# A gated dilated convolution on one core: one VectorE instruction put ahead of another, some products and half an output piece moved forward, and four stores in place of two

## The chip, the cores and the metric

The kernel runs on one core of one Trainium2 chip. The metric is device microseconds (us) of one execution; the time given for a kernel is the median of its runs.

## The reference

`x` has 2 batches of 16000 rows of 256 channels, in bf16. Three taps with a dilation of two rows make 512 channels from them; the first half goes through a tanh and the second through a sigmoid, the two are multiplied, and a 256 by 256 matrix makes the output.

```python
B, T, D, K = (2, 16000, 256, 3)
xp = pad(x, 4 rows ahead)
h = xp[t+4] @ w[0] + xp[t+2] @ w[1] + xp[t] @ w[2]
z = tanh(h[..., :256]) * sigmoid(h[..., 256:])
out = z @ w_o
```

## The kernel before, in words

**Tiles.** Rows are handled in groups. One group and two remainders (`extra`, `end`) of plain form compute the three taps directly (`direct`, L292). The other 15 groups are wide: 256 positions of 8 rows each, whose sums and differences (`q`, `qp`, `qm`, `qd`, made by VectorE and GpSimd at L213 to L231) let 14 products of 512 columns do the work of 24. Every group has four blocks, one for each 128 of the 512 channels, in the order tanh, sigmoid, tanh, sigmoid.

**A block.** A wide block B owns one `y` tile in PSUM (two banks, from a ring of three) and goes through these steps. `first` (L254, two products) fills bank 0 and ScalarE keeps it as `st` (`keep_first`, L276). `second` (L260, two products) adds to bank 0, and ScalarE keeps it as half of `sv` (`keep_second`, L280); GpSimd makes the other half of `sv` (`other`, L283). `third` (L263, two products) adds to bank 0, and VectorE makes bank 1 from bank 0 and `st` (`split_bank`, L286, called the split below). `late(B, 0)` (L268, four products) adds to both banks. VectorE subtracts `y` from `sv` (`rest`, L290). `late(B, 1)` (L271, four products) adds the last terms to both banks. ScalarE applies the function to `sv` (L332) and to `y` (L334). After two blocks VectorE multiplies tanh by sigmoid (the gate, L339).

**Output pieces.** A group's `z` gives pieces of 256 output rows each: `out_mm` (L364) does four products of 256 columns into one bank of the two-buffer ring `ps_o`, ScalarE evicts it to half of an `osb` tile (L401), and when both halves are there SyncE stores 256 KB (L374 or L381).

**Order of the work.** The whole order is written out by hand; each engine runs its instructions in program order, and the waits between engines follow from the tiles. The loop at L529 has one slot for each wide block, k = 4 to 63; slot 4 is called the first slot, slot 5 the second, slot 7 the fourth. In slot k TensorE does `late(V, 0)` of the block before (V), `second` of the slot's block (B), in the first six slots some products of the remainders (`extra_block`, L459, into `e_ps` tiles of the ring `ps_o`, two blocks of four still to come in slots 6 and 7; `plain_ends`, L467, in slots 8 and 9), then the output pieces that are due (`project`, L523: none up to slot 6, one in slots 7 to 9, two after), `first` of the next block (N), `third` of B, the other half of `first`, and `late(V, 1)`. Slot 5 (`early_second`) begins with `second` and holds both parts of `first` together.

VectorE's order within a slot: what `small` and `big` list for it (sums, differences, gates), `rest(V)`, in slot 7 alone one more sum from the list `mid` (L573; the sum `qm` of the next group, `wide_m`, L222), then the split of B; in slot 7 the gate of `extra` follows (L591). `other(B, last)` and the quarter differences (L234) on GpSimd wait for VectorE's latest listed instruction.

**The end.** Behind the loop (L613 on) come `late` of the last block, `project(2)`, and then four pieces of the group before, in two pairs (`left`): the first pair goes to a `y` tile and is evicted by VectorE, the second goes to `ps_o` and is evicted by ScalarE; each pair is stored in one transfer of 256 KB. Between and behind them stand the last gates (L620) and the last group's eight pieces, each stored singly (128 KB, L649), from both SyncE's and ScalarE's queue.

Of the kernel before, what the change touches and what calls it, by code (L numbers as in the profile page):

```python
# [13 lines left out]
def kernel(  # L14
# [37 lines left out]
    TAPS = (2, 0, 1)  # L52
# [16 lines left out]
    end = dict(wide=False, b=B - 1, r0=T // 4 - RE, R=RE, g="z")  # L69
    for g, G in enumerate(groups):  # L70
        G["g"] = g
    wides = [G for G in groups if G["wide"]]
    XW = RW + RH * max(len(G["parts"]) for G in wides)

# [13 lines left out]
    def new_y():  # L88
        return ps_y.tile([P, 2, BANK], f32, name="y")
# [8 lines left out]

    def load_plain(G):
        b, r0, R = G["b"], G["r0"], G["R"]  # L100
        xt = G["x"] = xt_pool.tile([P, 4, CT, RH + R], bf16, name=f"xt{G['g']}")
        if r0 == 0:
            nc.gpsimd.memset(xt[:, :, :, RH - 1:RH], 0.0)
            return
        nc.sync.dma_start_transpose(
            out=xt[:].rearrange("p j ct r -> p (j ct) r"),
            in_=x[b, 4 * (r0 - RH):4 * (r0 + R), :].rearrange("(r j) c -> r (j c)", j=4),
        )
# [142 lines left out]
    def first(B, ct):  # L251
        if ct == 0:
            B.y = new_y()
        nc.tensor.matmul(  # L254
            B.y[:, 0, :], lhsT=W["wmh"][:, ct, B.osl], rhs=B.G["qp"][:, :, ct, :],
            start=ct == 0, stop=ct == CT - 1, skip_group_check=True,
        )
# [4 lines left out]
    def third(B):  # L262
        mm(B, W["wm"], B.G["qm"][:, 1], 0)  # L263

    def late(B, n):
        G = B.G
        if n == 0:
            mm(B, W["wt"], G["q"][:, 1, 0], 0)  # L268
            mm(B, W["wu"], G["q"][:, 1, 1], 1)
        else:  # L270
            mm(B, W["wd2"], G["qd"][:, 0], 0)  # L271
            mm(B, W["wd0"], G["qd"][:, 1], 1)
# [12 lines left out]
    def split_bank(B):  # L285
        nc.vector.scalar_tensor_tensor(  # L286
            out=B.y[:, 1, :], in0=B.st[:], scalar=-0.5, in1=B.y[:, 0, :], op0=ALU.mult, op1=ALU.add)
# [67 lines left out]
            return G["z"][:, dt, WIDE_PLACE[jp], lo:lo + P]  # L355
        return G["z"][:, dt, 2 * jp + q, rb0:rb0 + P]

    def out_mm(G, rb0, jp, o_ps=None):
        if o_ps is None:
            o_ps = ps_o.tile([P, 2, D], f32, name="o_ps", tag="o_ps")  # L360
        G["o", rb0, jp] = o_ps
        for q in range(2):
            for dt in range(NT):
                nc.tensor.matmul(  # L364
                    o_ps[q] if isinstance(o_ps, list) else o_ps[:, q, :], lhsT=z_columns(G, rb0, jp, q, dt), rhs=wo_sb[:, dt, :],
                    start=(dt == 0), stop=(dt == NT - 1),
                )

    def store(G, rb0, js, osb, queue=None):

        queue = queue or nc.sync
        if not G["wide"]:
            t0 = 4 * G["r0"] + 4 * rb0
            queue.dma_start(out=out[G["b"], t0:t0 + 4 * P, :].rearrange("(p j) d -> p j d", j=4)[:, js, :], in_=osb[:])  # L374
            return
        row = 0
        for b, t0, rows in G["parts"]:
            lo, hi = max(rb0, row), min(rb0 + P, row + rows)
            if lo < hi:
                t = t0 + 8 * (lo - row)  # L380
                queue.dma_start(  # L381
                    out=out[b, t:t + 8 * (hi - lo), :].rearrange("(p j) d -> p j d", j=8)[:, js, :],
                    in_=osb[lo - rb0:hi - rb0],
                )
            row += rows

    def out_evict(G, rb0, jp, on_dve):
        o_ps = G["o", rb0, jp]
        copy = nc.vector.tensor_copy if on_dve else nc.scalar.copy
        if jp is None:  # L390
            te = 4 * G["r0"]
            osb = consts.tile([P, 2, D], bf16, name="osb_end")
            copy(out=osb[:], in_=o_ps)
            rows = out[G["b"], te:te + 4 * RE, :].rearrange("(r q h) d -> h r q d", q=2, h=2)
            for h in range(2):
                nc.sync.dma_start(out=rows[h], in_=osb[h * RE:(h + 1) * RE])
            return
        h = jp % 2
        if h == 0:
            G["osb"] = osb_pool.tile([P, 4, D], bf16, name="osb")  # L400
        copy(out=G["osb"][:, 2 * h:2 * h + 2, :], in_=o_ps)  # L401
        if h == 1:
            store(G, rb0, slice(2 * jp - 2, 2 * jp + 2), G["osb"])


    blocks = [Block(G, oi) for G in groups for oi in range(4)]
    extras = [Block(extra, oi) for oi in range(4)]
    ends = [Block(end, oi) for oi in range(4)]
    ND = 4
# [47 lines left out]
    last = wide_m(G0, 1)  # L457

    def extra_block(i, taps):  # L459
        E = extras[i]  # L460
        if TAPS[0] in taps:
            E.y = ps_o.tile([P, BANK], f32, name="e_ps", tag="o_ps")
        direct(E, taps, E.y[:])
        if TAPS[-1] in taps:
            activate(E, E.y[:])
# [17 lines left out]
    ready, todo, made = [], [], []  # L483
    small, big, mid = {}, {}, {}

    def do(steps, k):
        ins = None
        for step in steps.pop(k, []):
            ins = step() or ins
        return ins  # L490
# [32 lines left out]
    def project(n):  # L523
        for piece in todo[:n]:
            out_mm(*piece)
            made.append(piece)
        del todo[:n]

    for k in range(ND, NB):  # L529
        B, V = blocks[k], (blocks[k - 1] if k > ND else None)  # L530

        E = {
            ND: [(0, TAPS[2:]), (1, TAPS[:1])], ND + 1: [(1, TAPS[2:])], ND + 2: [(2, TAPS)],
            ND + 3: [(3, TAPS)],
        }.get(k, [])
        early_second = k == ND + 1
        if early_second:
            second(B)
            keep_second(B)
            extra_block(1, TAPS[1:2])  # L540
        if V:
            late(V, 0)
        if k >= ND + 2:
            Y = blocks[k - 2]
            activate(Y, "y")
            note_gates(Y, k)
        last = do(small, k) or last

        if k == ND + 6:
            todo.append(ready.pop())  # L550
        big_late = k == ND + 1

        def big_and_quarter(last):
            last = do(big, k) or last
            if B.oi == 0 and k > ND:
                quarter(B.G, 3, last)
            elif B.oi and not big_late and B.G["n"] + 1 < len(wides):
                for i in range(0 if k == ND + 2 else B.oi - 1, B.oi):
                    quarter(wides[B.G["n"] + 1], i, last)
            return last  # L560

        if not big_late:
            last = big_and_quarter(last)
        if not early_second:
            second(B)
            keep_second(B)
        if k == ND:
            for i in range(2, ND):
                activate(blocks[i], bank(blocks[i], i))
        other(B, last)  # L570
        if V:
            rest(V)
        last = do(mid, k) or last  # L573
        for e in E:
            extra_block(*e)
        if k in (ND + 4, ND + 5):
            plain_ends(*((ACT.Sigmoid, 1) if k == ND + 5 else (ACT.Tanh, 0)))

        project(0 if k < ND + 3 else 1 if k < ND + 6 else 2)
        evict()  # L580
        N = blocks[k + 1] if ND < k < NB - 1 else None

        split_first = k >= ND + 2
        if N:
            first(N, 0)
            if not split_first:
                first(N, 1)
        third(B)
        split_bank(B)
        if k == ND + 3:  # L590
            last = gates_of(extra, slice(0, 2))  # L591
        if big_late:
            last = big_and_quarter(last)
        if V:
            activate(V, "sv")
        if N:
            if split_first:
                first(N, 1)
            keep_first(N)
        if V:  # L600
            late(V, 1)
        todo += ready
        ready.clear()
        if B.oi == 0:
            if loaded_wide < len(wides):
                load_wide(loaded_wide)
                loaded_wide += 1
            if k == ND:
                load_end()
# [2 lines left out]

    Y, V = blocks[NB - 2:]  # L613
    G = V.G
    late(V, 0)
    activate(Y, "y")
    big.pop(NB)
# [5 lines left out]
    gate_phases(0, slice(0, 2), nc.gpsimd)  # L623
    rest(V)
    gate_phases(0, slice(2, 4))
    project(2)
    evict()


# [5 lines left out]
    left = [todo[i:i + 2] for i in range(0, len(todo), 2)]  # L635
# [17 lines left out]

    activate(V, "sv")
    two_pieces(left[0], "y")
    out_evict(*left[0][0], True)
    late(V, 1)
    gate_phases(1, slice(2, 4))
    activate(V, "y")
    out_evict(*left[0][1], True)  # L660
    two_pieces(left[1], "o")
    last_mm(0, (1, 2), "y")
    gate_phases(1, slice(0, 2))
    out_evict(*left[1][0], False)
    out_evict(*left[1][1], False)
    last_mm(P, (1, 2), "y")
    last_evict(0, (1, 2), (nc.sync, nc.sync))
    last_mm(0, (0, 3), "o")
# [35 lines left out]
```

## Time and profile before

| | |
|---|---|
| median of 3 runs | 263.51 us (263.49 to 263.56) |
| the profiled execution | 263.43 us |
| its span, first to last instruction | 261.6 us |
| mean granted TensorE clock | 0.996 |
| TensorE matmul busy | 256.0 us (98%) |
| ScalarE busy | 245.9 us (94%) |
| VectorE busy | 226.7 us (87%) |
| GpSimd busy | 112.8 us (43%) |

Times in rows are counted from the start of the span. PE is TensorE's matmul, PEld its weight load, DVE is VectorE, ACT is ScalarE, POOL is GpSimd, SP is SyncE. A row of the timeline has the start, the length, the engine, the line, the operation, the tile written and the tiles read, and `xN` where N instructions are merged. Matmuls are pipelined: the length of a row runs to the end of its last matmul, while the next one starts earlier, so the distance between the starts is what TensorE needs. On the other engines too a row can begin a few hundredths before the end of the one ahead of it.

### The profile page before, as it was taken

How to read it: one execution, taken by the hardware profiler on the slowest of the kernel's cores; microseconds unless marked ns; L12 is line 12 of the kernel's file. 1: busy time of each engine (PE TensorE's matmuls, PEld its weight loads, DVE VectorE, ACT ScalarE, POOL GpSimd, SP SyncE). 2: the span in 40 equal slices, each digit the busy share in tenths (PEclk: the TensorE clock that was granted, in tenths of full speed). 3: DMA queues.
4: the chain of work that ended last, by engine and by line, in shares of the span. 5: the costliest groups of instructions: out<-in, count | busy, mean ns of one | idle time of the engine just before them, and what ended most of it. 6: DMA issues, size and time to landing. Idle time of an engine off the chain costs nothing.

```text
span 261.6 us, 4231 instructions
## 1 busy us (share of the span) xinstructions
PE 256.0 (98%) x1464; PEld 144.2 (55%) x1464; DVE 226.7 (87%) x264; ACT 245.9 (94%) x378; POOL 112.8 (43%) x129
## 2 busy tenths in 40 slices
PE   8999999999999999999999999999999999999993
PEld 6644555555555555555555555555555555555562
DVE  2989969989889989999988988988988988986673
ACT  4668789999999999999999999999999999999993
POOL 1033434454453454355455355355345345444240
PEclk9999999999999999999999999999999999999998
DMA  7979073292834719256392934729274491221226
GB/s 209 201 177 192 0 180 94 83 209 83 175 119 123 209 52 212 111 117 174 96 175 105 199 120 103 203 79 215 81 169 124 101 231 43 80 83 40 82 80 241
DMA packets 79109, 35.10 MB, mean 134 GB/s; under 512 B 69232, under 2 KB 71536, under 8 KB 79088
## 3 DMA queue, kind: packets, MB, share of 16 engines
q1 hardware_dynamic: 77984, 33.92, 52.8%
q10 hardware_dynamic: 1104, 0.92, 1.1%
q8 instruction: 11, 0.18, 0.3%
q14 instruction: 10, 0.08, 0.1%
HBM read 1.18 MB, written 16.38 MB: 67 GB/s over the span
## 4 chain that ended last, share of the span: by engine, by line
PE 93%; DVE 3%; issue 1%; DMA 1%; ACT 0%; DVEq 0%; ACTq 0%
PE y L246 58%; PE o_ps L364 19%; PE y L254 9%; PE y L310 2%; PE y L140 1%; PE e_ps L310 1%; PE f_ps L310 1%; DVE sv L290 1%; DVE y L286 1%; DMA out_dram<-osb 1%; DVE qm L222 1%; PE wt_ps L171 0%; ACT osb L401 0%; PE y L364 0%; DVE osb L648 0%
## 5 line engine op out<-in xcount | busy, mean ns | idle before, releaser
L283 POOL TENSOR_TENSOR sv<-sv,st 128x512 f32<-128x512 f32 x60 | 76.4, 1274 | 23.9 <-ACT sv L280 22.2
L231 POOL TENSOR_TENSOR qd<-xq 128x256 bf16<-128x256 bf16 (+2 forms) x60 | 34.9, 585 | 114.2 <-DVE zw L339 55.4
L290 DVE TENSOR_TENSOR sv<-sv,y 128x1024 f32<-128x1024 f32 x60 | 72.7, 1212 | 3.8 <-PE y L246 3.7
L246 PE MATMUL y<-qd,wd_sb 128*128 128x512 bf16 x240 | 61.6, 379 | 0.1
L401 ACT CAST osb<-o_ps 128x512 bf16<-128x512 f32 x114 | 61.1, 591 | 0.2 <-PE o_ps L364 0.2
L286 DVE SCALAR_TENSOR_TENSOR y<-st,y 128x512 f32<-128x512 f32 x60 | 41.8, 696 | 21.9 <-PE y L246 19.6
L364 PE MATMUL o_ps<-wo_sb,zw 128*128 128x256 bf16 x450 | 58.4, 273 | 0.0
L364 PEld LDWEIGHTS <-zw 128*128 128x128 bf16 x480 | 47.0, 98 | 17.1
L254 PE MATMUL y<-qp,wmh_sb 128*128 128x512 bf16 x120 | 44.8, 379 | 0.0
L246 PEld LDWEIGHTS <-wd_sb 128*128 128x128 bf16 x240 | 23.5, 98 | 28.5 <-issue 0.6
L280 ACT ACTIVATE sv<-y 128x512 f32<-128x512 f32 x60 | 35.9, 598 | 1.4 <-PE y L246 1.1
L213 DVE TENSOR_TENSOR q<-xq 128x2048 bf16<-128x2048 bf16 (+2 forms) x32 | 36.8, 1155 | 0.0
L276 ACT ACTIVATE st<-y 128x512 f32<-128x512 f32 x60 | 36.3, 607 | 0.2 <-PE y L254 0.2
L246 PE MATMUL y<-q,wt_sb 128*128 128x512 bf16 x120 | 35.7, 379 | 0.2 <-DVE y L286 0.2
L246 PE MATMUL y<-qm,wph_sb 128*128 128x512 bf16 x120 | 35.7, 379 | 0.0
L246 PE MATMUL y<-qm,wm_sb 128*128 128x512 bf16 x120 | 35.7, 379 | 0.0
L246 PE MATMUL y<-q,wu_sb 128*128 128x512 bf16 x120 | 35.7, 379 | 0.0
L339 DVE TENSOR_TENSOR zw<-thw,sgw 128x2048 bf16<-128x2048 bf16 x28 | 34.1, 1217 | 0.0
L332 ACT ACTIVATE thw<-sv 128x1024 bf16<-128x1024 f32 x30 | 32.4, 1078 | 0.4 <-DVE sv L290 0.4
L332 ACT ACTIVATE sgw<-sv 128x1024 bf16<-128x1024 f32 x30 | 32.4, 1078 | 0.0
L334 ACT ACTIVATE sgw<-y 128x1024 bf16<-128x1024 f32 x30 | 31.3, 1043 | 0.1
L334 ACT ACTIVATE thw<-y 128x1024 bf16<-128x1024 f32 x30 | 31.3, 1044 | 0.0
(68 smaller groups left out, 178.8 us busy)
## 6 DMA issues: line engine op xcount, KB each, us to landing
out_dram<-osb SPq DMA_DIRECT2D x56, 256.0 KB, 2.1
out_dram<-osb SPq DMA_DIRECT2D x6, 128.0 KB, 2.2
w_sb<-in_w_dram ACTq DMA_DIRECT2D x2, 256.0 KB, 4.4
out_dram<-osb SPq DMA_DIRECT2D x2, 160.0 KB, 2.0
osb<-in_x_dram SPq DMA_DIRECT2D x1, 256.0 KB, 3.2
w_sb<-in_w_dram SPq DMA_DIRECT2D x1, 256.0 KB, 4.3
xq<-in_x_dram SPq DMA_TRANSPOSE x16, 7.2
out_dram<-osb ACTq DMA_DIRECT2D x2, 128.0 KB, 2.2
```

Of the source, the lines that this page charges most:

```text
L213: ins = nc.vector.tensor_tensor(out=sums(G, "q")[:, h, :, :, :, sl].rearrange("p h q ct r -> p h (q ct) r"), in0=s, in1=a, op=ALU.subtract ...
L246: nc.tensor.matmul(B.y[:, bank, :], lhsT=wmat[:, ct, B.osl], rhs=mv[:, :, ct, :], start=False, stop=ct == CT - 1, skip_group_check=True,)
L254: nc.tensor.matmul(B.y[:, 0, :], lhsT=W["wmh"][:, ct, B.osl], rhs=B.G["qp"][:, :, ct, :], start=ct == 0, stop=ct == CT - 1, skip_group_che ...
L276: nc.scalar.mul(B.st[:], B.y[:, 0, :], 4.0)
L280: nc.scalar.mul(B.sv[:, 0], B.y[:, 0, :], 2.0)
L283: after(nc.gpsimd.tensor_tensor(out=B.sv[:, 1], in0=B.sv[:, 0], in1=B.st[:], op=ALU.subtract), behind)
L286: nc.vector.scalar_tensor_tensor(out=B.y[:, 1, :], in0=B.st[:], scalar=-0.5, in1=B.y[:, 0, :], op0=ALU.mult, op1=ALU.add)
L290: nc.vector.tensor_tensor(out=B.sv[:], in0=B.sv[:], in1=B.y[:], op=ALU.subtract)
L332: nc.scalar.activation(out=dst[:, 2:4, :], in_=B.sv[:], func=func, scale=0.25)
L334: nc.scalar.activation(out=dst[:, 0:2, :], in_=B.y[:], func=func, scale=0.25)
L364: nc.tensor.matmul(o_ps[q] if isinstance(o_ps, list) else o_ps[:, q, :], lhsT=z_columns(G, rb0, jp, q, dt), rhs=wo_sb[:, dt, :], start=(dt ...
L401: copy(out=G["osb"][:, 2 * h:2 * h + 2, :], in_=o_ps)
```

## The change

There are four edits. (1) In slot 7 `do(mid, k)`, which is the sum `wide_m`, stands behind `split_bank(B)` instead of ahead of the remainder's products. (2) In slot 5 one half of `first` of block 6 (one product) stands ahead of `late(V, 0)`; the other half stays where it was. Of the remainder's block 2 the two products of the first tap stand at the end of slot 5, behind `third`, and of block 3 the two products of the first tap stand in slot 6; slots 6 and 7 do what is left of these blocks. (3) Behind the loop, half of the first output piece (two products of 256 columns) stands ahead of the last block's `late(V, 0)`, and its other half behind it. (4) The four pieces in `left` are stored singly as soon as each is evicted, 128 KB each.

```diff
-    def out_mm(G, rb0, jp, o_ps=None):
+    def out_mm(G, rb0, jp, o_ps=None, qs=(0, 1)):
...
-        for q in range(2):
+        for q in qs:
...
-    def out_evict(G, rb0, jp, on_dve):
+    def out_evict(G, rb0, jp, on_dve, single=False):
...
-        if h == 1:
+        if single:
+            store(G, rb0, slice(2 * jp, 2 * jp + 2), G["osb"][:, 2 * h:2 * h + 2])
+        elif h == 1:
             store(G, rb0, slice(2 * jp - 2, 2 * jp + 2), G["osb"])
...
-            ND: [(0, TAPS[2:]), (1, TAPS[:1])], ND + 1: [(1, TAPS[2:])], ND + 2: [(2, TAPS)],
-            ND + 3: [(3, TAPS)],
+            ND: [(0, TAPS[2:]), (1, TAPS[:1])], ND + 1: [(1, TAPS[2:])], ND + 2: [(2, TAPS[1:]), (3, TAPS[:1])],
+            ND + 3: [(3, TAPS[1:])],
...
             extra_block(1, TAPS[1:2])
+            first(blocks[k + 1], 0)
...
-        last = do(mid, k) or last
         for e in E:
             extra_block(*e)
...
         if N:
-            first(N, 0)
+            if not early_second:
+                first(N, 0)
             if not split_first:
                 first(N, 1)
         third(B)
+        if early_second:
+            extra_block(2, TAPS[:1])
         split_bank(B)
+        last = do(mid, k) or last
...
+    half = todo[0]
+    out_mm(*half, None, (0,))
     late(V, 0)
...
-    project(2)
+    out_mm(*half, half[0]["o", half[1], half[2]], (1,))
+    made.append(todo.pop(0))
+    project(1)
     evict()
...
-    out_evict(*left[0][0], True)
+    out_evict(*left[0][0], True, True)
...
-    out_evict(*left[0][1], True)
+    out_evict(*left[0][1], True, True)
...
-    out_evict(*left[1][0], False)
-    out_evict(*left[1][1], False)
+    out_evict(*left[1][0], False, True)
+    out_evict(*left[1][1], False, True)
```

## The prediction

> **What bounds the kernel now.** I read the page first: the busy shares and the chain of work that ended last.
>
> ```profile
> PE 256.0 (98%) x1464; PEld 144.2 (55%) x1464; DVE 226.7 (87%) x264; ACT 245.9 (94%) x378; POOL 112.8 (43%) x129
> ...
> PE 93%; DVE 3%; issue 1%; DMA 1%; ACT 0%; DVEq 0%; ACTq 0%
> ```
>
> TensorE carries 93% of the chain, so only time in which TensorE doesn't start a matmul can be won, unless matmuls go, and none do here. Next I asked for windows, to see whether the steady slots have such time: ten of them, 100.00 to 138.95.
>
> ```profile
> 100.00:138.95 38.95, 38.95 (x223) 21.52 (x221) 35.84 (x44) 38.95 (x61) 19.17 (x25) 1.00 0.68 152
> ```
>
> They have none: 38.95 of 38.95 us. A steady slot is 14 products of 512 columns and 8 of 256, which are worth 18 of 512, so ten slots are 180 such products and one takes 38.95 / 180 = 0.2164 us. I call that a unit; a product of 256 columns counts half. With it each stretch of TensorE's timeline can be checked: where two starts lie further apart than the units between them, TensorE waited. From the first slot on there are four such places of over 0.1 us, two in the second slot, one behind the fourth, one behind the loop. The end after the last matmul is stores.
>
> **The second slot.** TensorE's timeline there, then VectorE's, then one row of ScalarE's.
>
> ```profile
> 15.61 0.59 PE L246 MATMUL y<-qm,wm_sb 128*128 128x512 bf16 x2
> 16.04 0.59 PE L246 MATMUL y<-qm,wph_sb 128*128 128x512 bf16 x2
> 16.48 0.59 PE L310 MATMUL e_ps<-xte,w_sb 128*128 128x512 bf16 x2
> 17.06 0.59 PE L246 MATMUL y<-q,wt_sb 128*128 128x512 bf16 x2
> ...
> 18.79 0.59 PE L246 MATMUL y<-qm,wm_sb 128*128 128x512 bf16 x2
> 19.47 1.02 PE L246 MATMUL y<-qd,wd_sb 128*128 128x512 bf16 x4
> ```
> ```profile
> 16.31 0.69 DVE L286 SCALAR_TENSOR_TENSOR y<-st,y 128x512 f32<-128x512 f32 x1 [0.81 <-PE y L246]
> ...
> 18.19 1.22 DVE L290 TENSOR_TENSOR sv<-sv,y 128x1024 f32<-128x1024 f32 x1
> ```
> ```profile
> 15.90 0.60 ACT L336 ACTIVATE sg<-y 128x512 bf16<-128x512 f32 x1
> ```
>
> The remainder's two products (16.48) are done with at 16.48 + 2 units = 16.91; the late products start at 17.06, just behind the split (16.31 + 0.69 = 17.00). That is a wait of 0.15. `third` (18.79) ends its units at 19.22; the last late products start at 19.47, just behind `rest` (18.19 + 1.22 = 19.41), because they write the `y` that it reads. That is a wait of 0.25.
>
> The change puts one product of `first` into the first gap: the late products start at 16.91 + 0.22 = 17.13, past the split. The bank it fills is free, since the activation that read that buffer ended at 15.90 + 0.60 = 16.50; this cover is 0.41. These four units end at 18.00. Before, `rest` followed their end (17.06 + 4 units = 17.93) by 0.26, so now it starts at 18.26 and ends at 19.48, and the last late products may start 0.06 behind that, at 19.54. TensorE has until then two units of remainder 1, one of `first`, two of `third`, and the two moved products of remainder 2: 18.00 + 7 units = 19.51. So 0.03 of wait is left, the next slot starts four units later at 20.40 instead of 20.33, and two units (0.43) of its work are done. Sum: 0.43 - 0.07 = 0.36 won. The moved products issue no transfer and pass no queue. Their bank was last read by the activation of remainder 0, whose products end in the first slot. An unseen wait there is bounded by zero below and by the whole 0.36 above; I take zero, as the rows give every one of its inputs as ready.
>
> **The fourth slot.** TensorE, VectorE, GpSimd, and the same sum of VectorE's where GpSimd was idle.
>
> ```profile
> 27.91 0.59 PE L246 MATMUL y<-qm,wm_sb 128*128 128x512 bf16 x2
> 28.35 0.38 PE L254 MATMUL y<-qp,wmh_sb 128*128 128x512 bf16 x1
> 28.56 1.03 PE L246 MATMUL y<-qd,wd_sb 128*128 128x512 bf16 x4
> 29.76 0.59 PE L246 MATMUL y<-q,wt_sb 128*128 128x512 bf16 x2 [0.17 <-DVE y L286]
> ```
> ```profile
> 26.56 1.20 DVE L290 TENSOR_TENSOR sv<-sv,y 128x1024 f32<-128x1024 f32 x1
> 27.69 1.42 DVE L222 TENSOR_TENSOR qm<-q 128x1024 bf16<-128x1024 bf16 x1
> 29.03 0.68 DVE L286 SCALAR_TENSOR_TENSOR y<-st,y 128x512 f32<-128x512 f32 x1
> ...
> 31.36 1.21 DVE L290 TENSOR_TENSOR sv<-sv,y 128x1024 f32<-128x1024 f32 x1
> ```
> ```profile
> 27.29 1.27 POOL L283 TENSOR_TENSOR sv<-sv,st 128x512 f32<-128x512 f32 x1
> 31.52 0.61 POOL L231 TENSOR_TENSOR qd<-xq 128x256 bf16<-128x256 bf16 x1 [2.96 <-DVE zw L339]
> ```
> ```profile
> 14.21 0.69 DVE L222 TENSOR_TENSOR qm<-q 128x1024 bf16<-128x1024 bf16 x1
> ```
>
> The four late products (28.56) are done with at 29.43, and the next start at 29.76, behind the split, which ended at 29.71: a wait of 0.33. The split stood behind the sum (27.69, 1.42 long) though its input, `third`, was done with at 28.35. After the change the third slot starts at 20.40 and has 20 units (the moved remainder work cancels), so slot four starts at 24.73. Up to the end of `third` it has 15 units now: 27.98. In the first slot the split (16.31) followed the end of `third` (15.61 + 2 units = 16.04) by 0.27, so here it runs from 28.25 to 28.93. The slot's 20 units end at 29.06, where the next late products start without a wait; the cover is 0.07. Before it was 29.76: **0.70 won** in all, 0.15 + 0.25 + 0.33 less 0.03.
>
> What is queued behind the waiting split on VectorE: the sum, then two gates (29.71 to 31.36 before, 1.65 in all), then `rest`, for which the fifth slot's last late products wait. The sum takes 28.85 to 29.54 if it is as long as at 14.21, as GpSimd's subtraction, which follows slot four's `second`, ends 0.07 later than before, at 28.63. The gates end at 31.2, `rest` at 32.4. Ahead of those products TensorE has four late ones, two of `second`, six units of the other remainder, two of a piece and four of `first` and `third`: 29.06 + 18 units = 32.96, which is 0.56 behind `rest`; less the 0.06 that a start takes, the cover is 0.50. The sum's reader, `third` of the fifth slot, comes over two us after it. GpSimd's next instruction waits for the second gate (31.52), so it can't stand in the way between.
>
> The sum's length has two ends, 0.69 and 1.42. The 1.42 lay beside GpSimd's subtraction (27.29 to 28.56), the 0.69 beside nothing of GpSimd's; the moved sum starts behind the subtraction, so I take 0.69. With 1.42, `rest` would end at 33.13, the products would start at 33.19, 0.23 late, and the total (below) would be 263.0 instead of 262.76.
>
> The Trainium skill's page "SBUF — State Buffer", section "Who interferes with whom", says that a VectorE instruction with two SBUF inputs and a GpSimd instruction that reads SBUF exclude each other, the later one waiting for the other's end. The sum's end at 29.11, 0.55 behind GpSimd's, agrees. By that rule the sum gets its 0.69 at the new place, and the total stays.
>
> **Steady slots.** TensorE comes out of the fifth slot 0.70 ahead and needs ScalarE to follow, which was busy 38.95 of 38.95 too.
>
> ```profile
> 101.77 0.61 ACT L276 ACTIVATE st<-y 128x512 f32<-128x512 f32 x1
> ...
> 102.58 0.59 PE L246 MATMUL y<-qm,wph_sb 128*128 128x512 bf16 x2
> ```
>
> The `second` products must wait until ScalarE has read bank 0: it is done at 102.38, they start at 102.58: 0.20 of slack. In the moved slots I followed ScalarE's rows in the same way: the remainder's activations come two units earlier with their products, and its order is the same, so it keeps its distance to TensorE. I take no cost; rival (e) has the other end.
>
> **The end.** TensorE, VectorE, ScalarE, TensorE again, SyncE's issues, and the rate of the transfers (slices of 0.25 us from 252 on).
>
> ```profile
> 248.46 1.02 PE L246 MATMUL y<-qd,wd_sb 128*128 128x512 bf16 x4
> 249.48 0.59 PE L246 MATMUL y<-q,wt_sb 128*128 128x512 bf16 x2
> ```
> ```profile
> 248.73 0.70 DVE L286 SCALAR_TENSOR_TENSOR y<-st,y 128x512 f32<-128x512 f32 x1 [0.55 <-PE y L246]
> 250.60 1.22 DVE L290 TENSOR_TENSOR sv<-sv,y 128x1024 f32<-128x1024 f32 x1 [1.17 <-PE y L246]
> ```
> ```profile
> 251.94 1.07 ACT L332 ACTIVATE sgw<-sv 128x1024 bf16<-128x1024 f32 x1
> ```
> ```profile
> 253.82 1.91 PE L364 MATMUL y<-wo_sb,zw 128*128 128x256 bf16 x16
> ```
> ```profile
> 256.38 0.82 SPq L649 DMA_DIRECT2D out_dram<-osb  x2
> 258.29 0.39 SPq L649 DMA_DIRECT2D out_dram<-osb  x1
> ```
> ```profile
> GB/s 0 0 0 131 385 369 164 0 0 0 0 0 66 385 393 205 344 377 373 332 176 311 217 328 344 328 340 328 361 340 340 332 74 0 0 0 0 0 0 0
> ```
>
> TensorE is free at 248.46 + 4 units = 249.33 and waits 0.15 for the split (249.43). Half a piece is one unit: the late products start at 249.55 instead of 249.48, 0.07 late, with 0.22 done. But the last group's pieces (253.82) need the chain split, late products, `rest`, activation (done at 253.01), gate. It hangs on the late products and runs 0.07 later; the pieces, which TensorE could start 0.15 earlier, start at about 253.88. So the half piece wins nothing for those. It helps what stands between: the last four late products came 12 units behind 249.48, at 252.08, and now come as `rest` ends, at 250.67 + 1.22 + 0.06 = 251.95, so the last activation of `y`, and the ScalarE evictions behind it, start about 0.1 earlier.
>
> The single stores: SyncE issues two more, 0.39 each, ahead of the one at 256.38; nothing was moved from 253.75 to 255.00, so its queue has room there, and I cost them at nothing. The rate falls to 176 GB/s at 257.0, so the queue of transfers was nearly empty when the last seven of 128 KB came; from 257.5 to 260 they run at about 340 GB/s. Bytes sent earlier than that don't shorten this train. Its start follows ScalarE's evictions, about 0.1 earlier; its last members follow TensorE, up to 0.07 later. I take 0.05 won. The ends: 0.07 lost, or 0.38 won if one transfer of 128 KB at 340 GB/s drops out of the train.
>
> **Sum.** 263.43 - 0.70 - 0.05 = 262.68 for an execution like the profiled one. That one lies 0.08 under the median of 263.51, so the forecast is **262.76**.
>
> **Rivals.** (a) The end gains what its upper bound allows: 262.4. For it speaks that the rate stays at its level up to 260; against it the dip ahead. (b) The fourth slot's wait comes back as one for `rest`, the moved sum still 1.42 long: 263.0 as above. GpSimd would have to be in its subtraction until 28.9 or later. (c) The second slot's products only change which wait they stand beside, for instance the products of `first` waiting for their bank: 0.36 less, 263.1. Against it is the activation's end, 0.41 ahead. (d) The two more stores hold up SyncE's queue: 2 x 0.39 lost at the end, 263.5; the empty slices ahead of 255.00 speak against it. (e) Slower: ScalarE becomes the bound. It has no idle row in the steady slots; if its round came out longer than TensorE's 3.895 with the new phase, TensorE would lose that difference in each of the 54 slots k = 10 to 63. At 0.03 a slot that is 1.6, 264.4. It decides from 0.023 a slot, which makes up the 0.70 and the 0.53 that counts as slower. Against it are the 0.20 of slack and the same instructions in the same order.
>
> **Chances.** Forecast 0.64, (a) 0.07, (b) 0.08, (c) 0.07, (d) 0.04, (e) 0.10. A measurement of this kernel tells about 0.2%, 0.53 us, from no change, so faster means under 262.98. Forecast, (a) and half of (b), which lies on that line, make 0.75; the rest of (b), (c) and (d) make 0.15; (e) makes 0.10. The range reaches from (a), 262.35, to just past (c), 263.15, and leaves out (d), (e) and a little more.
>
> **What would show it.** Right: TensorE's starts in the slots k = 5 to 8 lie as far apart as their units, the fifth slot's first late products start at 29.06 +- 0.1, the split of the fourth slot stands ahead of a sum of 0.69, and every later slot starts 0.70 earlier than before, up to the loop's end; then the last group's pieces start 0.65 earlier, not 0.85. Wrong: a wait of TensorE for `rest` near 33 (b), for ScalarE in the second slot (c), in every steady slot (e), or a train of stores that ends more than 0.3 off from the rest.

## The result, and the profile after

The changed kernel takes 262.57 us (median of 9 runs, 262.42 to 263.31) against 263.51 before: a ratio of 0.9966, 95% interval [0.9958, 0.9975], or 0.66 to 1.11 us less. The forecast was 262.76, range 262.35 to 263.15. The profiled execution took 262.42 (263.43 before), its span is 260.6 (261.6 before). The share of the chain of work that TensorE carries went from 93% to 97%.

First TensorE's starts in the second slot, then VectorE's `rest` there.

```profile
16.41 0.59 PE L310 MATMUL e_ps<-xte,w_sb 128*128 128x512 bf16 x2
16.85 0.38 PE L254 MATMUL y<-qp,wmh_sb 128*128 128x512 bf16 x1
17.06 0.59 PE L246 MATMUL y<-q,wt_sb 128*128 128x512 bf16 x2
...
19.01 0.60 PE L310 MATMUL e_ps<-xte,w_sb 128*128 128x512 bf16 x2
19.47 1.02 PE L246 MATMUL y<-qd,wd_sb 128*128 128x512 bf16 x4
```
```profile
18.20 1.22 DVE L290 TENSOR_TENSOR sv<-sv,y 128x1024 f32<-128x1024 f32 x1
```

From 16.41 to 17.06 the starts lie three units apart, as many as there are products: the first wait is gone. The two moved products (19.01) end their units at 19.44, and the last late ones start at 19.47: 0.03 of wait is left, where 0.25 was. Now the fourth slot: TensorE, VectorE, GpSimd.

```profile
28.13 1.03 PE L246 MATMUL y<-qd,wd_sb 128*128 128x512 bf16 x4
28.99 0.59 PE L246 MATMUL y<-q,wt_sb 128*128 128x512 bf16 x2
...
32.90 1.03 PE L246 MATMUL y<-qd,wd_sb 128*128 128x512 bf16 x4
33.76 0.59 PE L246 MATMUL y<-q,wt_sb 128*128 128x512 bf16 x2
```
```profile
28.18 0.70 DVE L286 SCALAR_TENSOR_TENSOR y<-st,y 128x512 f32<-128x512 f32 x1 [0.51 <-ACT osb L401]
28.79 0.69 DVE L222 TENSOR_TENSOR qm<-q 128x1024 bf16<-128x1024 bf16 x1
...
31.13 1.22 DVE L290 TENSOR_TENSOR sv<-sv,y 128x1024 f32<-128x1024 f32 x1
```
```profile
27.20 1.27 POOL L283 TENSOR_TENSOR sv<-sv,st 128x512 f32<-128x512 f32 x1
```

28.13 and 28.99 are four units apart: the late products no longer wait. The split stands ahead of the sum, the sum begins 0.32 behind GpSimd's end at 28.47 and takes 0.69 instead of 1.42, and `rest` is done at 32.35, 0.55 ahead of the products that wait for it (32.90). The idle time ahead of the split names ScalarE's eviction (27.52 to 28.10), but `third`, from 27.48 on, explains it: its row ends at 28.07.

The end: TensorE, VectorE, ScalarE, and the rate in slices of 0.25 us from 251 on.

```profile
247.27 0.59 PE L246 MATMUL y<-qm,wm_sb 128*128 128x512 bf16 x2
247.70 1.02 PE L246 MATMUL y<-qd,wd_sb 128*128 128x512 bf16 x4
248.56 0.38 PE L364 MATMUL o_ps<-wo_sb,zw 128*128 128x256 bf16 x2
248.78 0.59 PE L246 MATMUL y<-q,wt_sb 128*128 128x512 bf16 x2
...
252.04 1.04 PE L364 MATMUL o_ps<-wo_sb,zw 128*128 128x256 bf16 x8
252.91 1.91 PE L364 MATMUL y<-wo_sb,zw 128*128 128x256 bf16 x16
```
```profile
249.90 1.22 DVE L290 TENSOR_TENSOR sv<-sv,y 128x1024 f32<-128x1024 f32 x1 [1.23 <-PE y L246]
...
252.25 0.69 DVE L628 TENSOR_TENSOR zw<-thw,sgw 128x1024 bf16<-128x1024 bf16 x1
```
```profile
250.06 1.07 ACT L401 CAST osb<-o_ps 128x512 bf16<-128x512 f32 x2
251.16 1.06 ACT L332 ACTIVATE sgw<-sv 128x1024 bf16<-128x1024 f32 x1
```
```profile
GB/s 0 0 0 16 377 369 287 0 53 340 131 0 0 106 348 197 336 185 344 193 328 201 328 230 344 336 328 352 344 336 340 336 258 0 0 0 0 0 0 0
```

The last group's pieces start at 252.91 instead of 253.82, 0.91 earlier. Of this, 0.06 is there before the first slot's `third` already (15.55 against 15.61), which the change doesn't touch; the other 0.85 is the value that the forecast ruled out when it gave 0.65. Between 248.56 and 252.91 TensorE has no wait left. The rate shows the single stores between 254.50 and 257.00, slices of 328 to 348 and of 185 to 230 GB/s in turn, and then the train of the last stores at 328 to 352 GB/s, as fast as before.

### The profile page after: what moved, and what is told of

Same layout as the page of the kernel before. It is cut to its first block, busy times and chain, and to the rows that moved or that the text cites. A ratio compares the mean times of both kernels' runs of the same rounds, so it can differ in the third digit from the quotient of the medians.

```text
span 260.6 us, 4235 instructions
## 1 busy us (share of the span) xinstructions
PE 255.4 (98%) x1464; PEld 144.0 (55%) x1464; DVE 225.9 (87%) x264; ACT 246.1 (94%) x378; POOL 112.9 (43%) x129
## 4 chain that ended last, share of the span: by engine, by line
PE 97%; DVE 0%; issue 0%; ACT 0%; DVEq 0%; ACTq 0%
PE y L246 60%; PE o_ps L364 19%; PE y L254 10%; PE y L310 2%; PE e_ps L310 2%; PE y L140 1%; PE y L364 1%; PE f_ps L310 1%; PE wt_ps L171 0%; DVE osb L658 0%; ACT osb L658 0%; PE tq L183 0%; PE tp L183 0%; DVEq L709 0%; DVE warm L127 0%
```

## The experiments

The eight others were timed against runs of the kernel before on the same chip (its median there 263.45 for the first four, 263.46 for the others). Executions of equal code differ by up to 0.6 us at the start alone (`third` of the first slot starts anywhere from 15.44 to 16.04 in these ten traces), so the totals separate little, and the distances between rows of one trace carry the argument. The last four columns are such distances, in us:

- slots: from the start of `third` in the first slot (k = 4) to the start of the late products of slot 9;
- to pieces: from `third` of the last slot to the start of the last group's pieces;
- to last landing: from the same `third` to the moment at which the last store has landed;
- to span's end: from that landing to the last instruction.

| kernel | median, us | ratio to before [95%] | slots | to pieces | to last landing | to span's end |
|---|---|---|---|---|---|---|
| before | 263.51 | | 18.92 | 5.79 | 12.57 | 1.03 |
| changed | 262.57 | 0.9966 [0.9958, 0.9975] | 18.21 | 5.64 | 12.47 | 0.91 |
| e1_split | 263.11 | 0.9987 [0.9978, 0.9996] | 18.58 | 5.79 | 12.57 | 1.04 |
| e2_products | 263.44 | 1.0 [0.9991, 1.0009] | 18.89 | 5.79 | 12.58 | 1.03 |
| e12_slots | 262.86 | 0.9975 [0.9964, 0.9986] | 18.21 | 5.79 | 12.57 | 1.04 |
| e34_end | 263.23 | 0.999 [0.9981, 0.9998] | 18.92 | 5.64 | 12.46 | 0.90 |
| e3_half | 263.36 | 0.9996 [0.9987, 1.0005] | 18.92 | 5.63 | 12.42 | 1.03 |
| e4_single | 263.24 | 1.0002 [0.9985, 1.002] | 18.92 | 5.79 | 12.57 | 0.91 |
| e_gate_first | 262.63 | 0.9969 [0.9958, 0.9981] | 18.21 | 5.72 | 12.48 | 0.90 |
| e_both_first | 262.82 | 0.9974 [0.9964, 0.9984] | 18.42 | 5.64 | 12.46 | 0.91 |

One of the 12 runs of `e4_single` took 266.06; it draws the ratio up to 1.0002, although the median is 0.22 under that of the runs beside it.

### Each slot's edit alone

`e1_split` has the first edit only, `e2_products` the second only, `e12_slots` both. Against the kernel before, the first and the second:

```diff
-        last = do(mid, k) or last
         for e in E:
...
         split_bank(B)
+        last = do(mid, k) or last
```
```diff
-            ND: [(0, TAPS[2:]), (1, TAPS[:1])], ND + 1: [(1, TAPS[2:])], ND + 2: [(2, TAPS)],
-            ND + 3: [(3, TAPS)],
+            ND: [(0, TAPS[2:]), (1, TAPS[:1])], ND + 1: [(1, TAPS[2:])], ND + 2: [(2, TAPS[1:]), (3, TAPS[:1])],
+            ND + 3: [(3, TAPS[1:])],
...
             extra_block(1, TAPS[1:2])
+            first(blocks[k + 1], 0)
...
-            first(N, 0)
+            if not early_second:
+                first(N, 0)
...
         third(B)
+        if early_second:
+            extra_block(2, TAPS[:1])
         split_bank(B)
```

> Of the four edits only the first: in slot 7 the split stands ahead of the sum. Theory (four waits of TensorE, each removed by its own edit where VectorE is free): the fourth slot starts as before at 24.66, its split follows third by 0.27 and ends at 29.3, TensorE is free at 29.42, so the 0.33 goes: late products at 29.42 instead of 29.76, total 0.33 less, 263.2. The waits at 17.06 and 19.47 stay. Rival (the sum and the gates, now behind the waiting split, make rest late): a wait of 0.2 to 0.3 ahead of the last late products near 33.4, total 263.4 to 263.5.

The slots are 0.34 shorter, the median is 0.34 under that of the runs beside it, and the interval does not reach 1. TensorE and VectorE in the fourth slot of this kernel, and TensorE in the fifth:

```profile
28.64 1.03 PE L246 MATMUL y<-qd,wd_sb 128*128 128x512 bf16 x4
29.50 0.59 PE L246 MATMUL y<-q,wt_sb 128*128 128x512 bf16 x2
...
33.19 0.38 PE L254 MATMUL y<-qp,wmh_sb 128*128 128x512 bf16 x1
33.41 1.03 PE L246 MATMUL y<-qd,wd_sb 128*128 128x512 bf16 x4
```
```profile
28.69 0.70 DVE L286 SCALAR_TENSOR_TENSOR y<-st,y 128x512 f32<-128x512 f32 x1 [0.85 <-ACT osb L401]
```

From 28.64 to 29.50 are four units and from 33.19 to 33.41 one: TensorE waits neither for the split nor, in the fifth slot, for `rest`. The rival is out.

> Only the second edit: products moved in slots 5 to 7, the split of slot 7 still behind the sum. Theory (the chain of VectorE binds slot 7: rest, sum held until GpSimd's subtraction ends, split, late products): slots 5 and 6 win 0.36 to 0.43 for TensorE, but the late products of slot 8 wait for the split, which comes no earlier than before, so they start at 29.7 to 29.85 as before and the total is within 0.1 of before, 263.5. Rival (edits add up, as a sum over TensorE's waits has it): 0.36 less, 263.15.

The slots are 0.03 shorter and the total is that of before. TensorE, VectorE and GpSimd:

```profile
28.14 1.03 PE L246 MATMUL y<-qd,wd_sb 128*128 128x512 bf16 x4
29.69 0.59 PE L246 MATMUL y<-q,wt_sb 128*128 128x512 bf16 x2 [0.52 <-DVE y L286]
```
```profile
27.61 1.42 DVE L222 TENSOR_TENSOR qm<-q 128x1024 bf16<-128x1024 bf16 x1
28.95 0.68 DVE L286 SCALAR_TENSOR_TENSOR y<-st,y 128x512 f32<-128x512 f32 x1
```
```profile
27.21 1.27 POOL L283 TENSOR_TENSOR sv<-sv,st 128x512 f32<-128x512 f32 x1
```

TensorE arrives at 28.14 + 4 units = 29.01, as early as in the changed kernel, and then waits 0.68 for a split that comes as late as ever: the sum, held up to GpSimd's end at 28.48, takes 1.42 again. Moving products ahead only made this wait longer (0.33 in the kernel before). The rival is out: the second edit is worth its 0.37 (18.58 to 18.21 in the table) only where the first has cleared the split.

> Edits one and two together, the end as before. Theory: slot 9 starts 0.70 earlier than before (0.77 by the profile of the changed kernel, of which 0.06 is the start-up), and the end keeps its waits, so the total is 0.70 less, 262.8, and the last group's pieces are 0.70 earlier. Rival (the end's edits make as much of the change's gain as these): 0.5 less or under, 263.0.

The slots take 18.21 as in the changed kernel, 0.71 less than before, and the end is that of before in all three columns. So 0.34 and 0.03 alone, 0.71 together.

### The end's edits

`e3_half` has the third edit only, `e4_single` the fourth only (the same in all four pieces), `e34_end` both. Against the kernel before, the third and the fourth:

```diff
+    half = todo[0]
+    out_mm(*half, None, (0,))
     late(V, 0)
...
-    project(2)
+    out_mm(*half, half[0]["o", half[1], half[2]], (1,))
+    made.append(todo.pop(0))
+    project(1)
```
```diff
-    out_evict(*left[0][0], True)
+    out_evict(*left[0][0], True, True)
```

> Edits three and four alone, slots 5 to 8 as before. Theory after the result (the half piece fills the wait of 0.15 and the last group's pieces follow, because the first product of a piece reads the half of z whose gate was earlier): the pieces start 0.14 earlier than before, the end 0.15 to 0.2 earlier, 263.3. Rival, the step of the prediction (pieces bound by the last gate, end 0.05 earlier): pieces 0.07 later, 263.45.

> Only the third edit: half a piece ahead of the last block's late products; left pieces stored in pairs. Theory: the pieces of the last group start 0.14 earlier than before as in the changed kernel, and the end with them, 0.1 to 0.15, 263.4. Rival (the single stores make the gain of the end): the same pieces, but the last transfer lands as before, 263.5.

> Only the fourth edit: the four left pieces stored singly. Theory: the train of the last seven transfers starts when its evictions do, so nothing changes, within 0.05, 263.5; the rate in the slices from 253 to 257 changes, the slice in which the last bytes go doesn't. Rival: 128 KB drop out of the train, the last bytes go up to 0.38 earlier, 263.15. Other rival: two more issues of 0.39 on SyncE hold up the last stores, 0.4 to 0.8 later.

The pieces come 0.15 earlier with the half piece, alone (5.63) or with the single stores (5.64), and not at all with the single stores alone (5.79). The last landing follows them: 0.15 earlier with the half piece alone, 0.11 with both, unchanged with the single stores alone. So the rivals of `e34_end` (pieces later) and of `e3_half` (the last transfer lands as before) are out. In the totals only `e34_end` differs from before; for the other two the total is inconclusive.

`e4_single` shows neither of its rivals, but its theory, that nothing changes within 0.05, doesn't hold either. Its last bytes go in the slice that begins at 259.75; those of the kernel before, whose last `third` starts 0.16 later, go in the slice that begins at 260.00. The last landing stands where it was, and yet the span ends 0.12 sooner behind it (0.91 against 1.03). This is so in all five kernels with single stores (0.90 or 0.91) and in none of the others (1.03 or 1.04). Where it comes from is told under "The stores" below. The rate of `e4_single`, slices of 0.25 us from 252 on:

```profile
GB/s 0 0 8 385 369 287 29 344 152 0 0 0 274 250 299 225 311 217 311 209 229 279 250 336 344 336 340 344 340 336 348 189 0 0 0 0 0 0 0 0
```

### Two chains, lengthened on purpose

`e_gate_first` is the changed kernel with the two products of each output half turned round in the first two pieces of the last group, so that the half of `z` with the last gate is read first.

```diff
-    last_mm(0, (1, 2), "y")
+    last_mm(0, (1, 2), "y", (1, 0))
...
-            for dt in range(NT):
+            for dt in dts:
...
-                    start=(dt == 0), stop=(dt == NT - 1),
+                    start=(dt == dts[0]), stop=(dt == dts[-1]),
```

> The changed kernel, with the order of the two products turned round in the first two pieces of the last group: the half of z whose gate is the last one is read first. Theory (in the changed kernel the pieces start at 252.91, 0.03 before the row of that gate ends, because their first product reads the other half): the pieces now wait for the gate and start about 0.06 behind its end, 0.05 to 0.1 later than in the changed kernel, total 262.6 to 262.7. Rival (the gate doesn't bind at all there): no change at the pieces, 262.57.

```profile
252.52 1.04 PE L364 MATMUL o_ps<-wo_sb,zw 128*128 128x256 bf16 x8
253.48 1.92 PE L364 MATMUL y<-wo_sb,zw 128*128 128x256 bf16 x16
```
```profile
252.73 0.69 DVE L628 TENSOR_TENSOR zw<-thw,sgw 128x1024 bf16<-128x1024 bf16 x1
```

TensorE is free at 252.52 + 4 units = 253.39 and starts at 253.48, 0.06 behind the gate's end (253.42). The distance to the pieces grows by 0.08. In the changed kernel the pieces start 0.03 before the gate's row ends (252.94), which the first product may, as it reads the other half of `z`. The last landing moves by 0.01 only (12.48 against 12.47), as SyncE's last issue is no later (10.16 behind the loop's last `third`, 10.19 in the changed kernel). The median is 0.06 above the changed kernel's, too little to tell.

`e_both_first` is the changed kernel with the other product of `first` moved too.

```diff
             first(blocks[k + 1], 0)
+            first(blocks[k + 1], 1)
```

> The changed kernel, with both products of first ahead of the late products in slot 5, one more than the wait of 0.15 holds. Theory (slot 5 is bound by late products, rest, late products; whatever stands ahead of the first of them moves the chain): the first late products start one unit, 0.22, later, rest too, the last late products wait 0.25 for it, and slots from 6 on are 0.22 later than in the changed kernel, total 262.8. Rival (TensorE's units alone count, the order ahead of the wait is free): no change, 262.57.

```profile
19.25 0.60 PE L310 MATMUL e_ps<-xte,w_sb 128*128 128x512 bf16 x2
19.92 1.02 PE L246 MATMUL y<-qd,wd_sb 128*128 128x512 bf16 x4
```
```profile
18.65 1.22 DVE L290 TENSOR_TENSOR sv<-sv,y 128x1024 f32<-128x1024 f32 x1 [0.27 <-PE y L246]
```

The slots grow by 0.21: VectorE now idles 0.27 ahead of `rest`, and TensorE waits from 19.68 to 19.92 for its end at 19.87. Its median is 0.25 above the changed kernel's, though the two intervals overlap. One product fits the wait; the second one delays the chain by its own length.

## Why the prediction was right, and where it wasn't

**Slots.** 0.70 forecast, 0.71 measured. Each step holds: the wait left in the second slot is 0.03 as worked out, the split follows `third` as in the first slot, the moved sum takes 0.69, `rest` has 0.55 to spare, and the steady slots keep the lead: slot 9 to the last slot's `third` takes 213.50 before and 213.51 after. Rivals (b), (c) and (e) show nowhere. One thing was told wrongly: the 0.70 stood as a sum of waits removed, each by its edit. The sum is right for all edits together only; `e2_products` shows that the second edit's share depends on the first.

**The half piece: wrong.** The prediction said that it "wins nothing" for the last group's pieces, which would start about 0.06 later; they start 0.15 earlier (5.64 against 5.79). The step that failed is that the pieces hang on the chain that ends with the gate. In the kernel before, TensorE's row ahead of the pieces and the gate were these:

```profile
252.95 1.04 PE L364 MATMUL o_ps<-wo_sb,zw 128*128 128x256 bf16 x8
```
```profile
253.04 0.69 DVE L620 TENSOR_TENSOR zw<-thw,sgw 128x1024 bf16<-128x1024 bf16 x1
```

TensorE was free at 252.95 + 4 units = 253.82, which is when the pieces started, and the gate had ended at 253.73. From 249.48 on TensorE had run 20 units in 4.34 us without a wait. So the pieces stood behind TensorE's own work, and filling its one wait of 0.15 moves them by 0.15, unless the gate becomes too late. Two terms made the forecast's gate too late. First, the activation was put behind `rest`. In the kernel before, ScalarE's evictions ran right up to it:

```profile
250.98 1.07 ACT L401 CAST osb<-o_ps 128x512 bf16<-128x512 f32 x2 [0.16 <-PE o_ps L364]
251.94 1.07 ACT L332 ACTIVATE sgw<-sv 128x1024 bf16<-128x1024 f32 x1
```

`rest` had ended at 251.82, the evictions' rows at 252.05; rows of ScalarE overlap by about 0.1, so the evictions set the start. The half piece lets them run earlier, and the activation follows `rest` by 0.04 instead of 0.12 (by 0.03 or 0.04 in all five traces with the half piece, by 0.12 in all five without). The gate is 4.98 behind the loop's last `third` instead of 5.01, not 0.07 later. Second, the first of a piece's products doesn't need the last gate, which gives up to half a unit, 0.11; `e_gate_first` shows this one by taking it away, and the pieces then start 0.08 later. The first reading rests on the rows alone; no run here changes the order of the evictions.

**The stores: the train as forecast, the cost not.** The forecast counted the two more issues and the earlier bytes at nothing. The earlier bytes are worth nothing, as it said: the last landing of `e4_single` is that of before. But two things were left out, a small loss and a larger gain.

The loss is in SyncE's queue of issues, which the forecast took to have room. In the changed kernel it has none: its last nine issues follow one another without a pause.

```profile
253.57 1.30 SPq L381 DMA_DIRECT2D out_dram<-osb  x3
254.96 2.90 SPq L659 DMA_DIRECT2D out_dram<-osb  x6
```

The last of them starts at 257.46, so they are 0.49 apart on average. 128 KB every 0.49 us is 267 GB/s, and the ten slices of the rate from 254.50 to 257.00 have a mean of 269: there the issues set the pace. In these traces an issue of SyncE's takes 0.33 after a pause and about 0.40 right behind another. SyncE's last issue comes 10.11 behind the loop's last `third` with the half piece alone, where the queue still has a pause, and 10.19 with the single stores too; the last landing goes from 12.42 to 12.47. This is the mechanism of rival (d), at a tenth of its price of 0.8.

The gain is behind the last landing. SyncE ends the program with five waits for landings, one after another in a fixed order. The view of waits counts those that found a store still under way (us in total, times, longest), first before, then changed:

```profile
SPq L699 <- DMA out_dram<-osb: 1.9, 2, 1.7
```
```profile
SPq L709 <- DMA out_dram<-osb: 1.7, 4, 0.8
```

Before, the second wait is the one that meets the last landing, and three more follow it, each 0.06 to 0.07 long. The stores count on eight semaphores in turn, so with two stores more the last landing is met by the fourth wait, and only one follows. Two waits fewer are 0.13, and 1.03 less 0.91 is 0.12. The order is read from the traces' semaphore records; the number agrees in all ten of them, but no run changes the waits alone. Nobody had planned this gain: it hangs on the number of stores, not on their size, and is luck. Rival (a) is out, as no transfer dropped out of the train.

**The account** of the spans, 0.99 (261.64 against 260.64): start-up 0.06, slots 0.71, last landing 0.10, closing waits 0.12. The forecast's 0.75 was 0.70 for the slots and 0.05 for the end. The slots were right, mechanism and size. The end was mis-sized: 0.22 in place of 0.05, since the half piece was put at a loss of 0.07 where it wins 0.15, and the closing waits weren't seen. The start-up isn't of the change.

## What to carry to other kernels

When one engine carries the chain, divide its steady stretch by its instructions and use that unit to find where its starts lie further apart: these gaps are what can be won, and work put ahead of a wait fills it only up to its length, since anything more delays the chain that the wait belongs to. Gaps that follow one another don't add up edit by edit; clear the one behind first, or the gain is given back there. For a chain at the end, ask of each start which of two rows that end close together released it, and which part of a tile the first instruction reads; and follow the trace past the last bytes to the last instruction, as waits there cost time too.

## What the runs showed of the hardware

The sum of two bf16 tiles in SBUF takes 0.69 by itself and 1.42 when it begins 0.40 into GpSimd's subtraction (27.61 against 27.21 to 28.48 in `e2_products`); it then ends 0.55 behind GpSimd. In the third slot of the kernel before, the same sum began 0.77 into a subtraction (24.45 against 23.68 to 24.95), took 1.04 and ended 0.54 behind GpSimd. That agrees with the Trainium skill, "SBUF — State Buffer", section "Who interferes with whom", where such a pair excludes each other. A sum that did nothing until GpSimd's end would have ended 0.69 behind it; the rows show 0.14 less, and why stays open.

The start-up up to the first slot varies by 0.6 us between executions of code that is the same there. That is as much as the 29 runs of the kernel before on one chip differ as a whole (263.25 to 263.88).
